# Attention and two expert layers on one core: stores one unit behind, some low parts on VectorE, two scratch tiles in SBUF, value products of a pair in three bursts

## The chip, the cores and the metric

The kernel runs on one core of one Trainium2 chip. The metric is the device time in microseconds (us); lower is better. The median of 3 runs before the change is 1033.18 us (1033.11 to 1035.49).

## The reference

The program is attention with a position bias, then a layer with a rational activation, then a layer with three products and a maximum. Batch 4, 8 heads, sequence 576, head size 64, so 2304 tokens of width 512.

```
scores = q @ k.T / 8 + bias(i, j, head)      # bias: a small two-layer net on log distances
attn   = exp(scores - max) / (sum + 1e-9)
x      = (attn @ v), heads side by side        # 2304 x 512
h      = x @ w_in                              # 2304 x 2048
g      = (a0 + a1 h + a2 h^2 + a3 h^3) / (1 + |b0||h| + |b1|h^2 + 1e-6)
x      = g @ w_out                             # 2304 x 512
h      = max(x @ w1, x @ w2, x @ w3)           # 2304 x 768
out    = h @ w_out2
```

The weights arrive as 64-bit floats and are narrowed on the chip.

## The kernel before

**Precision.** Most products run as three products of high and low parts (`F32R` tiles): ScalarE copies the high part, and GpSimd or VectorE subtracts it from the source to get the low part. A "low part" below is that one subtraction. The value products and the transposes run on plain F32.

**Order.** Nearly all instructions of all engines stand in the order in which the program writes them (`manual_schedule`), so each engine is a queue in order, and so is SP, which issues all DMAs. An instruction that waits holds up what is queued behind it on its engine.

**Stages.** First the bias is computed and stored (to about 70 us). Then the attention stage runs to about 335 us, drains into the first expert layer up to about 372 us, and the two layers follow (to about 745 us and to the end).

**Attention.** A unit is one batch, one pair of heads and one tile of 128 query rows (the fifth tile has 64, and both heads share its products). There are 80 units. A full pair takes five units, in two groups: query tiles 0 and 1, then 2, 3 and 4. The two first pairs of batch 0 run as groups [0], [1], [2] and [3, 4]. `attn_tick(n)` is one step: it issues the score products of unit n (`sc`), a burst of value products of an earlier group (`av`), the transposes of unit n - 2 (`T`), then VectorE's score reductions (`r0`, `r1`), the reciprocal and broadcast (`n`), the store of a finished group (`st`: VectorE multiplies the value bank by the reciprocals into an `xs` tile, and SP stores that to `x_d`), one step of early weight narrowing (`p1`), the splitting of key and query tiles on GpSimd (`sq1` and `sq`, from the list `sqq`), the exponentials (`e0`, `e1`) and the evacuation of the transposes (`v0`, `v1`).

**Value products.** A finished group is queued on `avq` in pieces of its five key blocks, one piece per step, due two steps later. Each key block has a product for each of the two heads, which write 64 partitions each, and each of these shows as two instructions in the trace. The pieces come from `CUT2` for a group of two units (3 and 2 blocks) and from `CUT3` for one of three (2, 2 and 1).

**Banks.** The PSUM tag `bank` has four buffers: the transposes take three of them in a unit, the value products one from their first piece to their store. In the first layer, `ffn_h` takes one for the hidden product `ph`, and `rat_poly` one for its scratch `s`; both are released when VectorE ends the rational function of that step. In the drain of attention, the first steps of the layer and the last units of attention are interleaved.

**Stores.** `attn_store` and `put` (the narrowed weights) issue their DMA on SP in the unit in which VectorE produces the data. `load_kq` and `load_v` for a later pair stand behind them in the same queue. `xs` has four buffers; the narrowed weights use the same tag.

**Low parts.** In `pair_stages`, `rest(i)` takes GpSimd for even and VectorE for odd blocks before the first layer starts. The weight pipeline starts in unit 64. In `split_x`, all low parts are GpSimd's.

Of the kernel before, what the change touches and what calls it, by code (L numbers as in the profile page):

```python
# [17 lines left out]
P = 128  # L18
# [8 lines left out]
HID = 32  # L27
TOFF = 572
TW = 1148
KN = {'AVL': 2, 'NSLOT': 35, 'NRAW': 3, 'NRAWX': 2, 'NATT': 4, 'HB': 0, 'NE': 'd', 'FP': 2, 'BL': 4, 'T4': 0, 'LSP': 1, 'KX': 4, 'HT': 'ss', 'EVP': 'da', 'TTP': 'dda', 'NXS': 4, 'EARLY': 4, 'NM0': 0, 'MAN': 3, 'MANF': 3, 'HA': 2, 'H0': [34, 35], 'L0': [(14, 'k2'), (18, 'v2'), (24, 'k3')], 'B4': 2, 'H2': [1, 2, 4, 6, 8, 10, 12, 14, 16], 'SP0': [3, 4], 'BW': 3, 'A2': ['na', 'sc', 'sq1', 'av', 'T', 'r0', 'r1', 'n', 'st', 'p1', 'p2', 'sq', 'e0', 'e1', 'v0', 'v1'], 'LL': 7, 'SL': 3, 'LL0': 9, 'SL0': 2, 'SQ': [1], 'CUT2': 2, 'CUT3': 3, 'WS': 14, 'WR': 41, 'EV': {None: 'da', 's': 'da', 'j': 'aa'}, 'WT': 64, 'XT': 8, 'XA': 3, 'XB': 8, 'F': ['g2a', 'g2d', 'h', 'g1a', 'w', 'g2p', 'g1d', 'g1p', 'y', 'x', 'g3'], 'LOW': 0, 'LOM': 3, 'LOI': 2, 'GHI': 'dve', 'GLO': 'dve', 'BED': 8, 'BE0': 16, 'NU1': 'pool', 'XE': ['act', 'pool'], 'RS': 3, 'PW': 1, 'WP': 10, 'NPK': 27, 'YSP': 'act', 'LAG': 2, 'EV1': 'dve', 'XSE': 'act', 'STQ': 'sp', 'PUQ': 'sp', 'NB0': 0, 'HP': 0, 'SB': 2, 'XLA': 3, 'XLB': 6, 'XSA': 11, 'YL': 4, 'MIX': [1, 2, 3], 'YN': [(6, 2), (6, 4), (6, 6), (7, 1), (7, 3), (7, 5), (8, 1), (8, 3), (8, 4), (8, 5)], 'WLOW': 1, 'YSN': {5: 2, 6: 2, 7: 1, 8: 1, 9: 1, 10: 1, 11: 1, 12: 1}, 'PLAN': [(2, 1, [0, 2, 3, 4, 5, 6, 7, 8]), (3, 1, [4, 6, 7, 8, 9, 10, 11, 12]), (4, 1, [8, 10, 11, 12, 13, 14, 15, 16]), (5, 2, [1, 3, 5, 6, 8, 10, 12, 14]), (6, 3, [0, 2, 3, 4, 5, 6, 7, 8]), (7, 3, [4, 6, 7, 8, 9, 10, 11, 12]), (8, 3, [8, 10, 11, 12, 13, 14, 15, 16]), (0, 4, [0, 2, 3, 4, 5, 6, 7, 8]), (1, 4, [6, 8, 9, 10, 11, 12, 13, 14])], 'WPN': {13: 1, 14: 1, 15: 1}, 'OB': [1, 5]}  # L30
REBIAS = 2.0 ** -112
TOSIGN = -2.0 ** 32
QC = 1.0 + 1e-6
# [4 lines left out]
def tile_attention_moe(  # L38
# [292 lines left out]
            pool.tensor_copy(*pair)  # L331

    avs = {}

    def attn_v(b, ts, p, js=range(5)):
        n = sum(P if t < 4 else 64 for t in ts)
# [15 lines left out]
    def attn_store(b, ts, p):  # L352
        po = avs.pop((b, ts[0], p))
        n = sum(P if t < 4 else 64 for t in ts)
        xs = sb.tile([P, 512], F32, tag="xs", name=f"xs{b}_{ts[0]}_{p}", bufs=KN['NXS'])
        dve.tensor_tensor(xs[:, :n], po[:, :n], at[b, ts[0], p][1][:, 1, :n], ALU.mult)  # L356
        tok = b * S + ts[0] * P
        (act if KN["STQ"] == "act" else sp).dma_start(x_d[:, p, tok:tok + n], xs[:, :n])


    wt_ = {}
# [17 lines left out]
    def weight_stages(src, name, n, packed=False, lo_eng=pool, narrow=None):  # L379
        box = {}  # L380
        wide_ = src.dtype != F32

        def load():
            if wide_:
                box["r"] = raw(f"wr{name}{n}", [P, 512, 2], I32)
                sp.dma_start(box["r"], src[n].bitcast(I32).rearrange("p (c w) -> p c w", w=2))
            else:
                box["r"] = raw(f"wr{name}{n}", [P, 512], F32)
                sp.dma_start(box["r"], src[n])

        def rebias():
            if wide_:
                low, high = box["r"][:, :, 0], box["r"][:, :, 1]
                act.activation(f32(high), f32(high), AF.Prelu, scale=REBIAS, alpha=TOSIGN)
                dve.tensor_scalar(low, low, 29, None, ALU.logical_shift_right)

        def join():
            if wide_:
                low, high = box["r"][:, :, 0], box["r"][:, :, 1]
                res = sb.tile([P, 512], I32, tag="xs", name=f"wn{name}{n}", bufs=KN['NXS'])  # L400
                dve.scalar_tensor_tensor(res, high, 3, low, ALU.logical_shift_left, ALU.bitwise_or)
                box["r"] = f32(res)

        def put():
            (act if KN["PUQ"] == "act" else sp).dma_start(narrow[n], box["r"])

        def high():
            weight_place(name, n, packed)
            r, w = box["r"], wt_[name, n]
            if isinstance(w, list):  # L410
                for k in range(4):
                    act.copy(w[0][k], r[:, k * P:(k + 1) * P])
            else:
                act.copy(w[:, 0:4].rearrange("p k c -> p (k c)"), r)

        def rest():
            r, w = box["r"], wt_[name, n]
            if isinstance(w, list):
                for k in range(4):
                    lo_eng.tensor_tensor(w[1][k], r[:, k * P:(k + 1) * P], f32(w[0][k]), ALU.subtract)  # L420
            else:
                hi, lo = (w[:, 4 * a:4 * a + 4].rearrange("p k c -> p (k c)") for a in range(2))
                lo_eng.tensor_tensor(lo, r, f32(hi), ALU.subtract)
            ready.add((name, n))

        if narrow is not None:
            return [load, rebias, lambda: (join(), put())]
        return [load, lambda: (rebias(), join()), high, rest]
# [4 lines left out]
    def pair_stages(src, name, n, packed):  # L433
        box = {}

        def load():
            box["r"] = raw(f"wp{name}{n}", [P, 2, 512], F32)
            sp.dma_start(box["r"], src[n:n + 2].rearrange("f p c -> p f c"))

        def high(i):  # L440
            weight_place(name, n + i, packed[i])
            r, w = box["r"][:, i], wt_[name, n + i]
            if isinstance(w, list):
                for k in range(4):
                    act.copy(w[0][k], r[:, k * P:(k + 1) * P])
            else:
                act.copy(w[:, 0:4].rearrange("p k c -> p (k c)"), r)

        def rest(i):
            r, w = box["r"][:, i], wt_[name, n + i]  # L450
            eng = low_eng(KN["LOI"], n + i) if not yps else pool
            if isinstance(w, list):
                for k in range(4):
                    eng.tensor_tensor(w[1][k], r[:, k * P:(k + 1) * P], f32(w[0][k]), ALU.subtract)
            else:
                hi, lo = (w[:, 4 * a:4 * a + 4].rearrange("p k c -> p (k c)") for a in range(2))
                eng.tensor_tensor(lo, r, f32(hi), ALU.subtract)
            ready.add((name, n + i))

        def wait():  # L460
            pass

        return [load] + [wait] * KN["PW"] + [
            lambda: high(0), lambda: (rest(0), high(1)), lambda: rest(1),
        ]

# [26 lines left out]
    def split_x(tag, blk, kc):  # L493
        n = blocks[blk][1]
        rt = xr[tag, blk, kc // 2]
        t = slot(f"{tag}s{blk}_{kc}", [P, 2, n], F32R)
        act.copy(t[:, 0], rt[:, kc % 2])
        pool.tensor_tensor(t[:, 1], rt[:, kc % 2], f32(t[:, 0]), ALU.subtract)  # L498
        xt[tag, blk, kc] = t

    PRODS = ((0, 0), (0, 1), (1, 0))
# [19 lines left out]
    def rat_poly(blk, f):  # L521
        n = blocks[blk][1]
        ph = ph_t[blk, f][:, :n]
        s = bank(f"s{blk}_{f}")[:, :n]
        if blk == 0 and f < KN["RS"]:
            bt = slot(f"g{blk}_{f}", [P, 2, 512], F32)
        else:
            if not gring:
                gring.append(big("gring", [P, 2, 2, 512]))
            bt = gring[0][:, len(gring) % 2]  # L530
            gring.append(None)
        q, u = bt[:, 0, :n], bt[:, 1, :n]
        bun[blk, f] = ph, s, q, u
        act.activation(s, ph, AF.Abs, scale=B0)  # L534
        act.activation(q, ph, AF.Square)  # L535
        dve.scalar_tensor_tensor(q, q, B1, s, ALU.mult, ALU.add)  # L536
        act.activation(u, ph, AF.Identity, scale=A3, bias=A2)  # L537
# [478 lines left out]
    def attn_tick(n):  # L1016
# [9 lines left out]
        for step in KN["A2"]:  # L1026
# [25 lines left out]
            elif step == "av":  # L1052
# [4 lines left out]
                        stq.append(av)  # L1057
                if u2 and u2[2] == u2[1][-1]:
                    av = (u2[0], u2[1], u2[3])
                    cuts = {1: (5,), 2: (3, 2), 3: (2, 2, 1)}  # L1060
                    cut = {1: (5,), 2: cuts[KN["CUT2"]], 3: cuts[KN["CUT3"]]}[len(u2[1])]
                    avq.extend((n + KN["AVL"], av, range(sum(cut[:k]), sum(cut[:k + 1]))) for k in range(len(cut)))
            elif step == "sq1":
# [8 lines left out]
        for b, p in loads_at.get(n, []):  # L1072
            if p % 2 == 0 and (b, p) not in vv:
                load_v(b, p)
            if (b, p) not in raws:
                load_kq(b, p)
        WT, XT = KN["WT"], KN["XT"]
        if WT <= n < NU:
            k = n - WT
# [10 lines left out]
    n = NU  # L1090
    with ordered(KN["MANF"]):
        while avq or stq or n < NU + KN['LAG']:
# [3 lines left out]
            ffn_tick(n - NU, "a")  # L1096
            n += 1
        ffn_tick(n - NU - 1, "b")
    n_drain = n - NU

    with ordered(KN["MANF"]):
# [95 lines left out]
```

## Time and profile before

| | before |
|---|---|
| median of 3 runs | 1033.18 us |
| the profiled execution | 1033.64 us |
| its span, first to last instruction | 1031.9 us |
| TensorE busy | 1000.2 us (97%) |
| VectorE busy | 745.4 us (72%) |
| ScalarE busy | 644.2 us (62%) |
| GpSimd busy | 517.6 us (50%) |
| DMA, mean | 167 GB/s |

The times come from one profiled execution. PE is TensorE, PEld its weight loads, DVE is VectorE, ACT is ScalarE, POOL is GpSimd, and SPq is SP's queue. A row of a timeline gives the start and the length of an instruction (or of several alike), its line in the kernel, what it writes and reads, and in brackets how long the engine sat idle just before, and what ended that.

### The profile page before, as it was taken

How to read it: one execution, taken by the hardware profiler on the slowest of the kernel's cores; microseconds unless marked ns; L12 is line 12 of the kernel's file. 1: busy time of each engine (PE TensorE's matmuls, PEld its weight loads, DVE VectorE, ACT ScalarE, POOL GpSimd, SP SyncE). 2: the span in 40 equal slices, each digit the busy share in tenths (PEclk: the TensorE clock that was granted, in tenths of full speed). 3: DMA queues.
4: the chain of work that ended last, by engine and by line, in shares of the span. 5: the costliest groups of instructions: out<-in, count | busy, mean ns of one | idle time of the engine just before them, and what ended most of it. 6: DMA issues, size and time to landing. Idle time of an engine off the chain costs nothing. (4 is left out here: it accounts for less than half of the span.)

```text
span 1031.9 us, 17512 instructions
## 1 busy us (share of the span) xinstructions
PE 1000.2 (97%) x6082; PEld 821.4 (80%) x6082; DVE 745.4 (72%) x1471; ACT 644.2 (62%) x1294; POOL 517.6 (50%) x691
## 2 busy tenths in 40 slices
PE   6899999999999899999999999999999999999998
PEld 2368767777776678788899788788799999999997
DVE  8976766777676789788889888788775545555544
ACT  8976777877787778777788778778731121131111
POOL 4035677877787354535636356559632641362111
PEclk9999999999999999999999999999999999999999
DMA  7978656565544342023141323323487557745701
GB/s 260 334 265 255 223 193 208 184 223 183 174 146 152 99 147 83 20 93 143 78 168 52 123 93 133 122 92 113 154 314 266 203 178 264 253 130 209 263 31 62
DMA packets 68872, 172.50 MB, mean 167 GB/s; under 512 B 6960, under 2 KB 24624, under 8 KB 68784
## 3 DMA queue, kind: packets, MB, share of 16 engines
q1 hardware_dynamic: 68784, 171.38, 48.0%
q8 instruction: 48, 0.79, 0.3%
q14 instruction: 40, 0.33, 0.1%
HBM read 124.83 MB, written 46.53 MB: 166 GB/s over the span
## 5 line engine op out<-in xcount | busy, mean ns | idle before, releaser
L506 PE MATMUL y<-gs,wwo 128*128 128x512 f32 (+1 forms) x940 | 213.4, 373 | 2.2 <-POOL gs L561 1.9
L506 PE MATMUL ph<-xs,wwi 128*128 128x512 f32 (+1 forms) x930 | 206.8, 370 | 3.0 <-POOL xs L498 1.8
L506 PEld LDWEIGHTS y<-gs,wwo 128*128 128x128 f32 x940 | 164.3, 188 | 37.9 <-POOL gs L561 4.9
L783 PE MATMUL pr<-yo,ws 128*128 128x384 f32 x875 | 190.7, 336 | 2.0 <-DVE m L772 2.0
L506 PEld LDWEIGHTS ph<-xs,wwi 128*128 128x128 f32 x930 | 162.2, 188 | 37.0 <-POOL xs L498 3.6
L561 POOL TENSOR_TENSOR gs<-gring,gs 128x512 fp32r<-128x512 f32 (+1 forms) x77 | 91.1, 1183 | 161.4 <-ACT gs L560 80.3
L783 PEld LDWEIGHTS pr<-yo,ws 128*128 128x128 f32 x875 | 155.4, 188 | 9.5 <-DVE m L772 5.2
L267 ACT ACTIVATE e<-e,st 128x576 f32<-128x576 f32 x144 | 110.8, 772 | 57.1 <-DVE st L261 44.3
L763 POOL TENSOR_TENSOR h<-m,h 128x384 fp32r<-128x384 f32 x36 | 36.7, 1018 | 162.7 <-ACT h L762 144.6
L261 DVE CUSTOM_DVE_ANT_0 e<-s,bias 128x576 f32<-128x576 f32 x144 | 103.6, 752 | 15.6 <-PE s L235 10.1
L534 ACT ACTIVATE s<-ph,keep 128x512 f32<-128x512 f32 (+1 forms) x80 | 49.5, 619 | 72.9 <-PE ph L506 72.5
L235 PE MATMUL s<-k,qs 128*128 128x288 f32 x512 | 84.9, 307 | 2.6 <-DVE st L261 1.4
L308 PEld LDWEIGHTS tp<-ident,e 128*128 128x128 f32 x564 | 60.5, 141 | 31.4 <-issue 11.3
L830 PE MATMUL o<-wmo,h 128*128 128x512 f32 x324 | 82.8, 393 | 0.0
L798 ACT COPY u<-pr 128x384 f32<-128x384 f32 x27 | 12.9, 479 | 109.1 <-PE pr L783 109.1
L308 PE MATMUL tp<-ident,e 128*128 128x128 f32 x564 | 78.5, 280 | 0.8 <-ACT at L1045 0.8
L350 PE MATMUL av<-at,v 128*64 128x320 f32 (+3 forms) x576 | 76.7, 391 | 1.7 <-DVE xs L356 1.1
L536 DVE SCALAR_TENSOR_TENSOR gring<-gring,keep,s 128x512 f32<-128x512 f32 (+1 forms) x77 | 53.0, 689 | 32.4 <-ACT gring L535 31.9
L235 PEld LDWEIGHTS s<-k,qs 128*128 128x128 f32 x512 | 70.3, 189 | 6.1 <-DVE st L261 3.3
L830 PEld LDWEIGHTS o<-wmo,h 128*128 128x128 f32 x324 | 60.1, 188 | 9.7
L548 DVE SCALAR_TENSOR_TENSOR gring<-gring,keep,s 128x512 f32<-128x512 f32 (+1 forms) x77 | 53.2, 691 | 16.6 <-ACT s L542 12.7
L191 PE MATMUL pb<-h,keep 128*32 128x288 f32 x576 | 48.4, 435 | 13.3 <-ACT bo L197 6.1
(168 smaller groups left out, 1895.4 us busy)
## 6 DMA issues: line engine op xcount, KB each, us to landing
ws<-ms_d SPq DMA_DIRECT2D x75, 512.0 KB, 4.8
ms_d<-wring SPq DMA_DIRECT2D x21, 512.0 KB, 2.6
bias_d<-bo SPq DMA_DIRECT2D x36, 288.0 KB, 6.7
kr<-in_k SPq DMA_DIRECT2D x16, 576.0 KB, 5.3
qr<-in_q SPq DMA_DIRECT2D x16, 576.0 KB, 5.7
bias<-bias_d SPq DMA_DIRECT2D x16, 576.0 KB, 6.1
nr<-in_m SPq DMA_DIRECT2D x18, 512.0 KB, 4.6
wrwin<-in_wi SPq DMA_DIRECT2D x16, 512.0 KB, 4.1
```

The costliest lines, as they stand in the source:

```text
L235: pe.matmul(pt[:, x, :HS], lhsT=qs[:, u, t * P:(t + 1) * P], rhs=ks[u][:, w, x * HS:(x + 1) * HS], start=w == 0, stop=w == 1,)
L261: dve.tensor_tensor_reduce(out=dst, in0=src, in1=bs, op0=ALU.add, op1=ALU.min, scale=-0.125, scalar=3.0e38, accum_out=st[:, u:u + 1],)
L267: act.activation(et[:, u], et[:, u], AF.Exp, bias=st[:, u:u + 1], scale=-1.0, accum_out=st[:, 2 + u:3 + u])
L308: pe.transpose(tp[:, j * P:(j + 1) * P], flat[:, 640 * u + j * P:640 * u + (j + 1) * P], ident)
L350: pe.matmul(po[r, :n], lhsT=l, rhs=m, start=j == 0, stop=j == 4, skip_group_check=True)
L506: pe.matmul(po, lhsT=wpart(key, a, k), rhs=rhs, start=first and i == 0, stop=last and i == 2)
L534: act.activation(s, ph, AF.Abs, scale=B0)
L536: dve.scalar_tensor_tensor(q, q, B1, s, ALU.mult, ALU.add)
L548: dve.scalar_tensor_tensor(u, u, A0, s, ALU.add, ALU.mult)
L561: pool.tensor_tensor(t[1], u, f32(t[0]), ALU.subtract)
L783: pe.matmul(pt, lhsT=w[:, a, ch * P:ch * P + P], rhs=ys[c][ch], start=ch == 0 and i == 0, stop=ch == 1 and i == 2,)
L830: pe.matmul(po, lhsT=h[:, a, (tt % 3) * P:(tt % 3 + 1) * P], rhs=mo_t[j][:, c], start=j == 0 and i == 0, stop=j == NF2 - 1 and i == 2,)
```

## The change

- `CUT2` goes from 2 to 1, and `CUT3` from 3 to 4, with a new entry in the table of cuts: a two-unit group is issued as one piece of 5 blocks, a three-unit group as pieces of 4, 0 and 1.
- `attn_store` and `put` no longer issue their DMA at once. They append it to `put_off`; `put_flush`, at the end of each `attn_tick`, issues the DMAs of the unit before and moves those of this unit to `put_due`.
- `rest(i)` uses VectorE while `sqq` still holds key and query splits, whatever the block's number.
- In `split_x`, the low part of block 0, part 3 goes to VectorE.
- In `rat_poly`, the scratch `s` of the first two steps (`RX` = 2) of block 0 is an SBUF tile of tag `xs`, not a bank.

```diff
-KN = {'AVL': 2,
+KN = {'RX': 2, 'AVL': 2,
...
-'CUT2': 2, 'CUT3': 3,
+'CUT2': 1, 'CUT3': 4,
...
+    put_off, put_due = [], []
+
+    def put_flush():
+        while put_due:
+            put_due.pop(0)()
+        put_due.extend(put_off)
+        put_off.clear()
...
     def attn_store(b, ts, p):
...
-        (act if KN["STQ"] == "act" else sp).dma_start(x_d[:, p, tok:tok + n], xs[:, :n])
+        put_off.append(lambda: sp.dma_start(x_d[:, p, tok:tok + n], xs[:, :n]))
...
         def put():
-            (act if KN["PUQ"] == "act" else sp).dma_start(narrow[n], box["r"])
+            put_off.append(lambda: sp.dma_start(narrow[n], box["r"]))
...
         def rest(i):
-            eng = low_eng(KN["LOI"], n + i) if not yps else pool
+            eng = pool if yps else dve if sqq else low_eng(KN["LOI"], n + i)
...
     def split_x(tag, blk, kc):
-        pool.tensor_tensor(t[:, 1], rt[:, kc % 2], f32(t[:, 0]), ALU.subtract)
+        (dve if blk == 0 and kc == 3 else pool).tensor_tensor(t[:, 1], rt[:, kc % 2], f32(t[:, 0]), ALU.subtract)
...
     def rat_poly(blk, f):
-        s = bank(f"s{blk}_{f}")[:, :n]
+        if blk == 0 and f < KN["RX"]:
+            s = sb.tile([P, 512], F32, tag="xs", name=f"s{blk}_{f}", bufs=KN['NXS'])
+        else:
+            s = bank(f"s{blk}_{f}")[:, :n]
...
-                    cuts = {1: (5,), 2: (3, 2), 3: (2, 2, 1)}
+                    cuts = {1: (5,), 2: (3, 2), 3: (2, 2, 1), 4: (4, 0, 1), 5: (5,)}
...
             if (b, p) not in raws:
                 load_kq(b, p)
+        put_flush()
...
+    put_flush()
+    put_flush()
     n_drain = n - NU
```

## Rows read from the trace of the kernel before

**Rows 1.** The page's busy time, share of the span and instructions of TensorE

```profile
PE 1000.2 (97%) x6082; PEld 821.4 (80%) x6082; DVE 745.4 (72%) x1471; ACT 644.2 (62%) x1294; POOL 517.6 (50%) x691
```

**Rows 2.** Busy by stretch: length, each engine's us (instructions), clock, DMA share, GB/s

```profile
71.50:116.00 44.50, 43.66 (x417) 38.12 (x417) 29.59 (x85) 32.42 (x80) 27.48 (x57) 1.00 0.74 241
116.00:195.00 79.00, 76.48 (x574) 57.63 (x571) 55.18 (x141) 59.27 (x145) 59.44 (x110) 1.00 0.57 196
195.00:300.00 105.00, 105.00 (x801) 80.77 (x798) 76.06 (x202) 82.51 (x197) 80.92 (x155) 1.00 0.55 184
300.00:335.00 35.00, 32.48 (x241) 23.73 (x239) 23.42 (x62) 27.56 (x66) 25.87 (x44) 1.00 0.44 145
```

**Rows 3.** Timeline of TensorE: two successive starts of score products, no value products between

```profile
68.43 1.31 PE L235 MATMUL s<-k,qs 128*128 128x288 f32 x8
...
70.58 1.30 PE L235 MATMUL s<-k,qs 128*128 128x288 f32 x8
```

**Rows 4.** Timeline of TensorE: score products, value bursts and the transposes behind them

```profile
285.48 1.30 PE L235 MATMUL s<-k,qs 128*128 128x288 f32 x8
...
300.17 1.52 PE L350 MATMUL av<-at,v 128*64 128x256 f32 x12
301.61 0.66 PE L308 MATMUL tp<-ident,e 128*128 128x128 f32 x4
...
302.24 1.30 PE L235 MATMUL s<-k,qs 128*128 128x288 f32 x8
303.47 0.65 PE L350 MATMUL av<-at,v 128*64 128x256 f32 x4
...
304.49 1.09 PE L308 MATMUL tp<-ident,e 128*128 128x128 f32 x8
...
305.55 1.30 PE L235 MATMUL s<-k,qs 128*128 128x288 f32 x8
```

**Rows 5.** Timeline of TensorE, 150 to 350 us: instructions behind which a wait stands

```profile
151.81 0.33 PE L315 MATMUL tt<-ident,rb 128*128 128x128 f32 x1 [1.20 <-POOL rb L278]
...
154.05 1.30 PE L350 MATMUL av<-at,v 128*64 128x320 f32 x8 [0.85 <-DVE xs L356]
...
314.17 0.33 PE L315 MATMUL tt<-ident,rb 128*128 128x128 f32 x1 [1.15 <-POOL rb L278]
...
327.53 1.30 PE L350 MATMUL av<-at,v 128*64 128x320 f32 x8 [0.47 <-ACT at L1045]
...
339.44 0.73 PE L506 MATMUL ph<-xs,wwi 128*128 128x512 f32 x2 [1.56 <-POOL xs L498]
...
347.26 3.06 PE L506 MATMUL ph<-xs,wwi 128*128 128x512 f32 x12 [1.05 <-DVE g L550]
```

**Rows 6.** Timeline of SP's queue before the query load for batch 1, pair 2

```profile
134.40 0.38 SPq L386 DMA_DIRECT2D wrwin<-in_wi  x1
139.50 0.32 SPq L405 DMA_DIRECT2D wi_n<-wnwin  x1
...
142.05 0.38 SPq L129 DMA_DIRECT2D qr<-in_q  x1
```

**Rows 7.** Timeline of GpSimd where that query load lands

```profile
149.84 1.04 POOL L140 TENSOR_SCALAR qs<-qr 128x1024 fp32r<-128x1024 f32 x1 [4.06 <-DMA qr<-in_q]
```

**Rows 8.** Line 457, the weight low parts: min/median/max ns, first and last start

```profile
L457 POOL TENSOR_TENSOR wwi<-wpwi,wwi x8: 1275/1285/1317, 290.4 to 361.5; 128x512 fp32r<-128x512 f32 x8
...
L457 DVE TENSOR_TENSOR wwi<-wpwi,wwi x6: 680/686/1737, 293.0 to 347.1; 128x512 fp32r<-128x512 f32 x6
...
L457 DVE TENSOR_TENSOR wwo<-wpwo,wwo x2: 1289/1378/1468, 299.9 to 312.5; 128x512 fp32r<-128x512 f32 x2
```

**Rows 9.** Groups by line: ScalarE's exponentials and evacuation (busy us, mean ns, idle before)

```profile
L267 ACT ACTIVATE e<-e,st 128x576 f32<-128x576 f32 x144 | 110.8, 772 | 57.1 <-DVE st L261 44.3 <-POOL qtail L155 5.8 <-DVE st L276 3.2
...
L1045 ACT COPY at<-tp 128x512 f32<-128x512 f32 x78 | 44.8, 575 | 3.9 <-PE av L350 2.5 <-PE tp L308 0.3
...
L267 ACT ACTIVATION_READ_ACCUMULATOR e<-e,st 128x1 f32 x144 | 27.2, 189 | 0.0
```

More of the change, by code (lines that the diff above doesn't have):

```diff
@@ L29 @@
 TW = 1148
-KN = {'AVL': 2, 'NSLOT': 35, 'NRAW': 3, 'NRAWX': 2, 'NATT': 4, 'HB': 0, 'NE': 'd', 'FP': 2, 'BL': 4, 'T4': 0, 'LSP': 1, 'KX': 4, 'HT': 'ss', 'EVP': 'da', 'TTP': 'dda', 'NXS': 4, 'EARLY': 4, 'NM0': 0, 'MAN': 3, 'MANF': 3, 'HA': 2, 'H0': [34, 35], 'L0': [(14, 'k2'), (18, 'v2'), (24, 'k3')], 'B4': 2, 'H2': [1, 2, 4, 6, 8, 10, 12, 14, 16], 'SP0': [3, 4], 'BW': 3, 'A2': ['na', 'sc', 'sq1', 'av', 'T', 'r0', 'r1', 'n', 'st', 'p1', 'p2', 'sq', 'e0', 'e1', 'v0', 'v1'], 'LL': 7, 'SL': 3, 'LL0': 9, 'SL0': 2, 'SQ': [1], 'CUT2': 2, 'CUT3': 3, 'WS': 14, 'WR': 41, 'EV': {None: 'da', 's': 'da', 'j': 'aa'}, 'WT': 64, 'XT': 8, 'XA': 3, 'XB': 8, 'F': ['g2a', 'g2d', 'h', 'g1a', 'w', 'g2p', 'g1d', 'g1p', 'y', 'x', 'g3'], 'LOW': 0, 'LOM': 3, 'LOI': 2, 'GHI': 'dve', 'GLO': 'dve', 'BED': 8, 'BE0': 16, 'NU1': 'pool', 'XE': ['act', 'pool'], 'RS': 3, 'PW': 1, 'WP': 10, 'NPK': 27, 'YSP': 'act', 'LAG': 2, 'EV1': 'dve', 'XSE': 'act', 'STQ': 'sp', 'PUQ': 'sp', 'NB0': 0, 'HP': 0, 'SB': 2, 'XLA': 3, 'XLB': 6, 'XSA': 11, 'YL': 4, 'MIX': [1, 2, 3], 'YN': [(6, 2), (6, 4), (6, 6), (7, 1), (7, 3), (7, 5), (8, 1), (8, 3), (8, 4), (8, 5)], 'WLOW': 1, 'YSN': {5: 2, 6: 2, 7: 1, 8: 1, 9: 1, 10: 1, 11: 1, 12: 1}, 'PLAN': [(2, 1, [0, 2, 3, 4, 5, 6, 7, 8]), (3, 1, [4, 6, 7, 8, 9, 10, 11, 12]), (4, 1, [8, 10, 11, 12, 13, 14, 15, 16]), (5, 2, [1, 3, 5, 6, 8, 10, 12, 14]), (6, 3, [0, 2, 3, 4, 5, 6, 7, 8]), (7, 3, [4, 6, 7, 8, 9, 10, 11, 12]), (8, 3, [8, 10, 11, 12, 13, 14, 15, 16]), (0, 4, [0, 2, 3, 4, 5, 6, 7, 8]), (1, 4, [6, 8, 9, 10, 11, 12, 13, 14])], 'WPN': {13: 1, 14: 1, 15: 1}, 'OB': [1, 5]}
@@ new lines @@
+KN = {'RX': 2, 'AVL': 2, 'NSLOT': 35, 'NRAW': 3, 'NRAWX': 2, 'NATT': 4, 'HB': 0, 'NE': 'd', 'FP': 2, 'BL': 4, 'T4': 0, 'LSP': 1, 'KX': 4, 'HT': 'ss', 'EVP': 'da', 'TTP': 'dda', 'NXS': 4, 'EARLY': 4, 'NM0': 0, 'MAN': 3, 'MANF': 3, 'HA': 2, 'H0': [34, 35], 'L0': [(14, 'k2'), (18, 'v2'), (24, 'k3')], 'B4': 2, 'H2': [1, 2, 4, 6, 8, 10, 12, 14, 16], 'SP0': [3, 4], 'BW': 3, 'A2': ['na', 'sc', 'sq1', 'av', 'T', 'r0', 'r1', 'n', 'st', 'p1', 'p2', 'sq', 'e0', 'e1', 'v0', 'v1'], 'LL': 7, 'SL': 3, 'LL0': 9, 'SL0': 2, 'SQ': [1], 'CUT2': 1, 'CUT3': 4, 'WS': 14, 'WR': 41, 'EV': {None: 'da', 's': 'da', 'j': 'aa'}, 'WT': 64, 'XT': 8, 'XA': 3, 'XB': 8, 'F': ['g2a', 'g2d', 'h', 'g1a', 'w', 'g2p', 'g1d', 'g1p', 'y', 'x', 'g3'], 'LOW': 0, 'LOM': 3, 'LOI': 2, 'GHI': 'dve', 'GLO': 'dve', 'BED': 8, 'BE0': 16, 'NU1': 'pool', 'XE': ['act', 'pool'], 'RS': 3, 'PW': 1, 'WP': 10, 'NPK': 27, 'YSP': 'act', 'LAG': 2, 'EV1': 'dve', 'XSE': 'act', 'STQ': 'sp', 'PUQ': 'sp', 'NB0': 0, 'HP': 0, 'SB': 2, 'XLA': 3, 'XLB': 6, 'XSA': 11, 'YL': 4, 'MIX': [1, 2, 3], 'YN': [(6, 2), (6, 4), (6, 6), (7, 1), (7, 3), (7, 5), (8, 1), (8, 3), (8, 4), (8, 5)], 'WLOW': 1, 'YSN': {5: 2, 6: 2, 7: 1, 8: 1, 9: 1, 10: 1, 11: 1, 12: 1}, 'PLAN': [(2, 1, [0, 2, 3, 4, 5, 6, 7, 8]), (3, 1, [4, 6, 7, 8, 9, 10, 11, 12]), (4, 1, [8, 10, 11, 12, 13, 14, 15, 16]), (5, 2, [1, 3, 5, 6, 8, 10, 12, 14]), (6, 3, [0, 2, 3, 4, 5, 6, 7, 8]), (7, 3, [4, 6, 7, 8, 9, 10, 11, 12]), (8, 3, [8, 10, 11, 12, 13, 14, 15, 16]), (0, 4, [0, 2, 3, 4, 5, 6, 7, 8]), (1, 4, [6, 8, 9, 10, 11, 12, 13, 14])], 'WPN': {13: 1, 14: 1, 15: 1}, 'OB': [1, 5]}
```

## The prediction

> **What bounds the kernel now.** First the page's busy times: TensorE is busy for 97% of the span [rows 1]. Then the busy times by stage [rows 2]: between 71.5 and 335 us, the attention stage, TensorE is busy for 257.6 of 263.5 us, while VectorE, ScalarE and GpSimd stand at 62 to 79%. So what TensorE is given to do sets the time there, and only two things shorten it: less time per unit on TensorE, and fewer waits of TensorE. The reader should see that the stage isn't uniform: in 195 to 300 us TensorE never rests (105.00 of 105.00), in 116 to 195 it rests 2.5 us and in 300 to 335 another 2.5 [rows 2]. After 372 us nothing is edited, and I let that part shift as a whole.
>
> Third, TensorE's timeline, from the start of one unit's score products to the start of the next. A unit without value products takes 2.15 us (68.43 to 70.58) [rows 3]. A unit with eight value instructions of 256 columns takes 3.31 us (302.24 to 305.55). Its burst lasts 1.02 us (303.47 to 304.49), and a burst of twelve lasts 1.44 us (300.17 to 301.61), so one instruction adds (1.44 - 1.02) / 4 = 0.105 us [rows 4]. Eight of them are 0.84 us, and 3.31 - 2.15 - 0.84 leaves **0.32 us that each burst costs whatever its length**. It is paid going from the 128-column form to the 64-column form and back, and it counts as busy.
>
> Fourth, the waits of TensorE [rows 5]: 1.20 and 0.85 us at 151 to 154; five waits from 314.17 to 327.53 (the first and the last stand there; 1.15, 0.23, 0.30, 0.34 and 0.47, together 2.49 us); 1.56 us at 339.44; 1.05 us at 347.26.
>
> **The change part by part.** *Bursts.* A full pair has 5 units and, today, 5 bursts (3+2 key blocks for the two-unit group, 2+2+1 for the three-unit group). With one cut of 5 and cuts of 4, 0 and 1 it has 3; the empty one issues nothing. 14 full pairs save 2 bursts each, and the two early pairs save 1 each in their last group: 30 bursts. 30 x 0.32 = 9.6 us. The columns stay. Where TensorE sets the pace all of that is gained; where it already waits for others I count half. The stretches 71.5 to 116 and 195 to 300 are 149.5 of 263.5 us, the other two 114 [rows 2], so (149.5 + 114 / 2) / 263.5 = 0.78, and 0.78 x 9.6 = 7.5 us. Bounds: half of it, 4.8, to all, 9.6.
>
> *The uneven units that come with it.* Following the queue of bursts, the unit of query tile 1 now has all five blocks (20 instructions), that of tile 2 none, tile 3 four blocks, tile 4 none, and the next tile 0 the last block. About 28 units are thus as short as 2.15 us. No row shows such a unit in mid-stage, so I bound what it loses. Below: nothing, as in rows 3, where a short unit ran without a wait. Above: it lasts as long as ScalarE's work of a unit, 2 x (0.772 + 0.189) + 2 x 0.575 = 3.07 us [rows 9], 0.92 us more, 28 x 0.92 = 25.8 us in all. I stay near the lower end. The short unit always stands beside one with 16 or 20 value instructions, in which ScalarE and VectorE catch up before the transposes. In the tile 2 unit no value bank is held, so its three transpose banks have a fourth beside them; the tile 4 unit has one exponential instead of two. A long burst also frees the transposed tile a unit earlier than today. I take 2.0 us lost (0.07 us for each).
>
> *Stores one unit behind.* SP is a queue in order. At 139.50 it issues the narrow-weight store for which it had waited on VectorE, and only then the loads of v, k and q; the q load goes out at 142.05 [rows 6]. GpSimd waits 4.06 us for it, until 149.84 [rows 7], then runs late, and TensorE waits 1.20 us for GpSimd's broadcast and 0.85 us for what VectorE does behind that [rows 5]. With that store and the attention stores a unit later, their data is long there when SP reaches them, and the loads queued behind them follow what SP issued at 134.40 [rows 6] or the release of their buffer, which the rows don't separate. Each microsecond earlier up to 2.05 counts. Bounds 0 to 2.05; I take 1.5. What now waits instead is the store's buffer: four tiles, under one new one per unit, each held one unit longer (3.3 us). I cost that at nothing; VectorE's multiply would wait if a fifth were wanted early.
>
> *Low parts on VectorE.* Three weight low parts fall in units in which key and query splits are queued (67, 71 and 72) and leave GpSimd, 1.28 us each. On VectorE they took 0.69 us, or 1.29 to 1.47 in two cases [rows 8]. VectorE is busy 23.4 of 35 us there [rows 2], so it has room, but they stand ahead of the next unit's score reduction. GpSimd's broadcast is what is late at 314.17 [rows 5]. Bounds for the five waits: from 1.0 us worse (three long low parts, a third of each on the path) to 2.49 better; I take 1.0. The fourth is the low part of the last x tile of the first block. TensorE waits 1.56 us for it at 339.44 [rows 5], since GpSimd does a weight low part of 1.28 us first. VectorE is free once ScalarE has written the high part. Bounds 0 to 1.56; I take 0.8, because it may hit a long 1.3 us case.
>
> *The first two rational steps in SBUF.* At 347.26 the third hidden product waits 1.05 us for VectorE to release a bank [rows 5]; two steps hold four banks beside the value products. Two scratch tiles leave the banks, and so does the value tile, one unit sooner. What is late next is the low part of the first activated tile for the first output product. Bounds 0 to 1.05; I take 0.8. The four VectorE operations with that scratch I cost at nothing, hidden beside a hidden product; without that cover they lose up to 0.78 us each (1.47 - 0.69 [rows 8]).
>
> The Trainium skill speaks against these two edits. By its page "SBUF — State Buffer" (Who interferes with whom), a VectorE instruction with two SBUF inputs and a GpSimd instruction that reads SBUF exclude each other for their whole length. The 1.47 us case agrees with that, the 0.69 us median doesn't, and the rows don't show what ran beside either. By the rule alone these two parts would gain nothing.
>
> *Sum.* 7.5 + 1.5 + 1.0 + 0.8 + 0.8 = 11.6 us gained, 2.0 lost, 9.6 net. The profiled execution took 1033.64 us (span 1031.9); 1033.64 - 9.6 = 1024.0. The median of the runs is 0.46 below the profiled one, so **1023.6 us**.
>
> **The rivals.** *A, slower: the short unit is paced by ScalarE.* Then the transposes of the short units wait for evacuations. At the full 3.07 us the 28 units lose 25.8 us, against 11.6 gained: 14.2 us slower, 1047. It decides against the change from 11.6 / 28 = 0.41 us per short unit. For it: ScalarE is busy 79% in 300 to 335 [rows 2], and conversions come on top. Against it: the neighbouring long units and the short unit of rows 3. *B, absorbed: the slack of the others is smaller than their busy shares suggest,* since they wait for each other in order. Then bursts pay only in 195 to 300 us, 105 / 263.5 x 9.6 = 3.8 us, and the waits stay: 1029.4. For it: TensorE already waits in both neighbouring stretches. Against: those waits have causes of their own [rows 5 to 7]. *C, the two units compared differ by more than a burst,* so that the 0.32 us isn't removed. Then only the waits pay, 4.1 - 2.0 = 2.1 us: 1031.1. Against it: the burst alone already has 1.02 - 0.84 = 0.18 us that don't grow with its length [rows 4]. *D, low parts and scratch exclude GpSimd:* the last three terms, 2.6 us, are lost: 1026.2.
>
> **How the numbers follow.** Forecast, a gain of 5 to 16 us: 0.70. A 0.08, B 0.11, C 0.05, D 0.06. A measurement of this kernel can't tell 0.3% (3.1 us) from no change. The forecast and D are faster; of B and C together, 0.09 is faster and 0.07 the same; of A, 0.06 is slower, and 0.02 is the same; that makes faster 0.85, same 0.09, slower 0.06. The range: all bounds at their best give 9.6 + 2.05 + 2.49 + 1.56 + 1.05 = 16.8 us, 1016.4; I set the low end at 1017.5. The high end takes in B and just about C: 1031.
>
> **What would show it.** The value bursts of the attention stage number 50, not 80, and a full pair takes 16.1 us, not 16.76 (285.48 to 302.24 [rows 4]). Units without value products last 2.15 to 2.3 us; at 2.6 or more, A is at work. The q loads go out sooner behind the units' stores, GpSimd's waits for them shrink, and the waits at 151 to 154 go. The first hidden product runs through with at most 0.8 us of waiting, and the third starts without VectorE. The stage from 372 us on keeps its length. The prediction is wrong if transposes or scores wait in the short units, or if a full pair takes as long as before.

## The result, and the profile after

| | before | after |
|---|---|---|
| median | 1033.18 us | 1023.0 us (1020.06 to 1024.71) |
| profiled execution | 1033.64 us | 1020.06 us |
| its span | 1031.9 us | 1018.2 us |

The ratio is 0.9889 (95% interval 0.9869 to 0.9908): 1.1% faster. (The two medians alone give 0.9901, inside that interval.) The same kernel beside other runs of before gave 1020.72 us and 0.9865 (0.9843 to 0.9887). The forecast was 1023.6 us. The profiled execution is the fastest of its five, so its trace shows 13.6 us where the medians show 10.2.

The page's busy times of the changed kernel answer [rows 1]:

```profile
PE 991.0 (97%) x6082; PEld 823.6 (81%) x6082; DVE 750.0 (74%) x1475; ACT 644.1 (63%) x1294; POOL 514.9 (51%) x687
```

TensorE has 9 us less of busy time for the same 6082 instructions. The busy times by stage answer [rows 2]; the stage ends 10 us sooner, so the last two stretches are moved by that:

```profile
71.50:116.00 44.50, 44.50 (x430) 39.77 (x428) 30.20 (x86) 32.48 (x79) 28.14 (x59) 1.00 0.71 239
116.00:195.00 79.00, 78.22 (x611) 61.62 (x607) 60.41 (x155) 64.04 (x156) 62.53 (x118) 1.00 0.65 211
195.00:290.00 95.00, 95.00 (x751) 76.68 (x750) 70.59 (x188) 76.34 (x184) 76.02 (x143) 1.00 0.57 188
290.00:325.00 35.00, 33.07 (x248) 25.50 (x244) 26.50 (x66) 30.17 (x71) 26.66 (x45) 1.00 0.47 152
```

In 116 to 195 us TensorE now rests 0.8 us instead of 2.5 and issues 611 instructions instead of 574. TensorE's timeline in mid-stage answers [rows 3, 4]:

```profile
234.26 1.40 PE L246 MATMUL s<-k,qtail 128*128 128x288 f32 x10
...
243.73 1.30 PE L235 MATMUL s<-k,qs 128*128 128x288 f32 x8
...
250.53 1.41 PE L246 MATMUL s<-k,qtail 128*128 128x288 f32 x10
...
257.06 1.95 PE L357 MATMUL av<-at,v 128*64 128x256 f32 x16
258.84 0.60 PE L357 MATMUL av<-att,vz 128*64 128x256 f32 x4
...
260.00 1.30 PE L235 MATMUL s<-k,qs 128*128 128x288 f32 x8
...
262.14 1.04 PE L235 MATMUL s<-k,qs 128*128 128x288 f32 x6
```

A full pair takes 16.27 us (243.73 to 260.00, or 234.26 to 250.53 between the score products of tile 4) instead of 16.76 [rows 4]. The unit after the five-block burst starts at 260.00 and the next at 262.14: a short unit of 2.14 us in mid-stage, as long as that of [rows 3].

A yardstick for all runs below: the starts of the tile 4 score products (line 246) give the lengths of the 14 full pairs, from the second early pair to the last one.

| kernel | ratio to before (95%) | 14 pairs, us | inner 11, us | disturbed pairs of the inner 11 |
|---|---|---|---|---|
| before | 1 | 241.4 | 189.3 | 5 (17.16 to 19.18; undisturbed 16.76) |
| changed kernel | 0.9889 (0.9869 to 0.9908) | 230.0 | 180.9 | 1 (17.82; undisturbed 16.2 to 16.3) |
| cuts alone | 1.0009 (0.9994 to 1.0024) | 242.0 | 188.0 | 5 (17.14 to 18.57) |
| stores alone | 0.9958 (0.9944 to 0.9971) | 236.8 | 184.6 | none |
| cuts and stores | 0.9926 (0.9910 to 0.9942) | 233.0 | 180.9 | 1 (17.97) |
| changed, stores at once | 0.9962 (0.9947 to 0.9976) | 239.3 | 188.7 | 6 (16.74 to 18.58) |

The inner ones leave out the first two, which still hold bursts of the early pairs, and the last; a pair counts as disturbed from about 0.35 us above the undisturbed length. The lengths come from one trace of each kernel; a gain in us that stands beside a ratio is worked out from that ratio.

Of the 13.6 us between the profiled executions, 11.5 lie in these 14 pairs. About 0.8 lies ahead of them: the first scores start at 61.77 instead of 62.80, and in 50 to 71.5 us the granted clock of the execution before was 0.92, that after 1.00. The edits act behind that part, and in the second trace of the changed kernel the first scores start at 62.67. About 1.3 lie behind the last scores.

### The profile page after: what moved, and what is told of

Same layout as the page of the kernel before. It is cut to its first block, busy times and chain, and to the rows that moved or that the text cites. A ratio compares the mean times of both kernels' runs of the same rounds, so it can differ in the third digit from the quotient of the medians.

```text
span 1018.2 us, 17475 instructions
## 1 busy us (share of the span) xinstructions
PE 991.0 (97%) x6082; PEld 823.6 (81%) x6082; DVE 750.0 (74%) x1475; ACT 644.1 (63%) x1294; POOL 514.9 (51%) x687
## 5 line engine op out<-in xcount | busy, mean ns | idle before, releaser
L261 DVE CUSTOM_DVE_ANT_0 e<-s,bias 128x576 f32<-128x576 f32 x144 | 103.8, 752 | 13.6 <-PE s L246 8.9
L357 PE MATMUL av<-at,v 128*64 128x320 f32 (+3 forms) x576 | 70.1, 385 | 0.0
```

The source lines that it names most:

```text
L261: dve.tensor_tensor_reduce(out=dst, in0=src, in1=bs, op0=ALU.add, op1=ALU.min, scale=-0.125, scalar=3.0e38, accum_out=st[:, u:u + 1],)
L357: pe.matmul(po[r, :n], lhsT=l, rhs=m, start=j == 0, stop=j == 4, skip_group_check=True)
```

## The experiments

**Is a burst worth something by itself?** The kernel before with the cuts alone.

```diff
-'CUT2': 2, 'CUT3': 3,
+'CUT2': 1, 'CUT3': 4,
```

> The kernel before with the cuts 5 and 4, 0, 1 alone. Theory (each burst costs TensorE a constant beside its columns): a full pair goes from 16.76 to about 16.25 us where TensorE sets the pace, 14 pairs, so 6 to 8 us faster, about 1026, and the waits of TensorE at 151 to 154 and after 314 us stay. Rival (the gain comes from the earlier loads, and the cuts only shift columns): within 2 us of before. Rival A (short units paced by ScalarE): slower than before, short units of 2.6 us and more.

Measured: 1035.6 us beside 1034.88, 0.1% slower, with an interval that holds no change. The cuts alone give nothing. Undisturbed pairs did fall to 16.2 us, but others rose to 17 to 18.6. TensorE's waits in its timeline:

```profile
115.19 0.33 PE L315 MATMUL tt<-ident,rb 128*128 128x128 f32 x1 [1.60 <-POOL rb L278]
...
123.32 0.33 PE L315 MATMUL tt<-ident,rb 128*128 128x128 f32 x1 [1.00 <-POOL rb L278]
...
259.96 0.33 PE L315 MATMUL tt<-ident,rb 128*128 128x128 f32 x1 [1.00 <-POOL rb L278]
```

In the trace of the kernel before, no wait for that broadcast stands at any of these three places. Ahead of the third, SP's queue:

```profile
235.17 0.38 SPq L386 DMA_DIRECT2D wrwon<-in_wo  x1
240.89 0.32 SPq L405 DMA_DIRECT2D wo_n<-wnwon  x1
241.31 0.38 SPq L121 DMA_DIRECT2D v<-in_v  x1
241.78 0.41 SPq L127 DMA_DIRECT2D kr<-in_k  x1
242.40 0.33 SPq L129 DMA_DIRECT2D qr<-in_q  x1
```

and GpSimd's timeline:

```profile
249.41 1.05 POOL L140 TENSOR_SCALAR qs<-qr 128x1024 fp32r<-128x1024 f32 x1 [2.32 <-DMA qr<-in_q]
```

It is the pattern of [rows 6, 7] at another place: SP stands for 5.7 us in front of a store of narrowed weights, then issues v, k and q at once; GpSimd waits 2.32 us for q, runs late with its splits, and its broadcast for TensorE comes late behind them. The inner 11 pairs lose 9.7 us against an undisturbed length of 16.21, where before they lost 4.9 against 16.76: that takes back most of the 6.0 us that the bursts save in them. That a shorter pair leaves less time for the loads is the likely reason, but it is argued: GpSimd's own waits for the query loads are no longer than before (8.5 us instead of 9.8 in 71 to 335 us), while TensorE's waits for GpSimd's broadcast grow from 2.3 us to 5.2.

**What are the earlier loads worth?** The kernel before with only the stores one unit behind.

```diff
...
-        (act if KN["STQ"] == "act" else sp).dma_start(x_d[:, p, tok:tok + n], xs[:, :n])
+        put_off.append(lambda: sp.dma_start(x_d[:, p, tok:tok + n], xs[:, :n]))
...
-            (act if KN["PUQ"] == "act" else sp).dma_start(narrow[n], box["r"])
+            put_off.append(lambda: sp.dma_start(narrow[n], box["r"]))
...
+        put_flush()
...
```

> The kernel before with only the stores one unit behind. Theory: GpSimd's waits for the query loads (9.8 us in all) shrink to about 1 us and TensorE's waits at 151 to 154 (2.05 us) go; 1.5 to 2 us faster, about 1031.5; the length of a full pair elsewhere stays 16.76 us. Rival (the loads are the main gain): 5 us or more. Rival (loads are hidden anyway): 0.

Measured: 1030.96 beside 1034.88, 0.42% faster (4.4 us), three times the forecast. In 71 to 335 us GpSimd waits for no query load any more. Pairs that were disturbed now have the undisturbed length; from its timeline:

```profile
155.38 1.40 PE L246 MATMUL s<-k,qtail 128*128 128x288 f32 x10
...
172.14 1.40 PE L246 MATMUL s<-k,qtail 128*128 128x288 f32 x10
```

That is 16.76 us. The pair at the same place in the kernel before:

```profile
156.34 1.40 PE L246 MATMUL s<-k,qtail 128*128 128x288 f32 x10
...
163.64 1.48 PE L235 MATMUL s<-k,qs 128*128 128x288 f32 x8 [0.23 <-DVE st L261]
...
173.97 1.40 PE L246 MATMUL s<-k,qtail 128*128 128x288 f32 x10
```

It took 17.63 us, and the 0.23 us in brackets is all the waiting that is shown in it. The brackets miss much of what a pair loses; its length doesn't.

**Do the cuts pay on top of the stores?** Both edits, nothing else.

> The kernel before with the cuts and the stores one unit behind, nothing else. Alone the cuts gave 0.0% and the stores 0.4%. Theory (the cuts shorten a pair by 0.5 us only if GpSimd gets the keys and queries in time, which the early loads give): the two together give about 4.4 + 6.5 us less the late wait at 312 and 314, so 9 to 10.5 us, about 1025 beside 1034.9; full pairs of 16.2 to 16.3 us. Rival (the parts add): 4.4 us, 1030.5.

Measured: 1027.42 beside 1034.89, ratio 0.9926. The cuts that gave nothing alone give 0.3% more on top of the stores (0.9958 to 0.9926); the 14 pairs fall from 236.8 to 233.0. That is 7.7 us in all (6.0 to 9.3 by the interval): the rival (4.4 us) is out, but the 9 to 10.5 us weren't reached either. The trace says where they are missing:

```profile
302.07 1.40 PE L246 MATMUL s<-k,qtail 128*128 128x288 f32 x10
...
306.80 0.33 PE L315 MATMUL tt<-ident,rb 128*128 128x128 f32 x1 [1.19 <-POOL rb L278]
...
323.32 1.40 PE L246 MATMUL s<-k,qtail 128*128 128x288 f32 x10
...
332.28 0.73 PE L514 MATMUL ph<-xs,wwi 128*128 128x512 f32 x2 [2.13 <-POOL xs L506]
```

The last pair takes 21.25 us, and the x part is waited for 2.13 us: the late stretch, in which the weight low parts load GpSimd. With the low parts on VectorE, in the changed kernel, the same pair:

```profile
299.36 1.43 PE L246 MATMUL s<-k,qtail 128*128 128x288 f32 x10
...
301.57 0.66 PE L308 MATMUL tp<-ident,e 128*128 128x128 f32 x4 [0.29 <-ACT at L1055]
...
302.25 1.30 PE L235 MATMUL s<-k,qs 128*128 128x288 f32 x8
...
309.40 1.30 PE L235 MATMUL s<-k,qs 128*128 128x288 f32 x8
...
312.20 1.48 PE L235 MATMUL s<-k,qs 128*128 128x288 f32 x8 [0.40 <-DVE st L261]
...
317.52 1.40 PE L246 MATMUL s<-k,qtail 128*128 128x288 f32 x10
```

18.16 us, 3.1 less.

**Which store holds the loads up?** As the run before, but the narrowed weights are stored at once and only the attention stores wait a unit.

```diff
-            put_off.append(lambda: sp.dma_start(narrow[n], box["r"]))
+            (act if KN["PUQ"] == "act" else sp).dma_start(narrow[n], box["r"])
```

> As the run before, but only the attention stores go one unit behind; the stores of the narrowed weights are issued at once. Theory (the query loads stand behind the narrowed store in the same unit, as at 139.5 us before): most of the waits of the cuts alone come back up to 260 us, pairs of 17 to 18.5 us, about 1030. Rival (the attention stores hold the loads up): as the run before, about 1025.

Measured: 1032.31 beside 1034.89, ratio 0.9977 (0.9963 to 0.9991), 14 pairs of 241.0 us: most of the gain is gone, and pairs of 17.05 to 18.6 us are back. What waited for whom in 71 to 335 us (total, times, longest):

```profile
POOL qs L140 <- DMA qr<-in_q: 7.4, 5, 3.7
...
PE tt L315 <- POOL rb L278: 4.3, 5, 1.2
```

In the changed kernel the first of these is 1.2 us in all and the second doesn't occur. So the loads stand above all behind the store of the narrowed weights, as long as weights are narrowed. A kernel with only that store late wasn't run, so what the attention stores add isn't shown.

**The changed kernel without the late stores.**

> The changed kernel with the stores issued at once, as before. If the parts simply add, it is 1.5 to 2 us slower than the changed kernel (about 1025). If shorter units make the loads more urgent, more than that: 3 us or more, with GpSimd's waits for the query loads well above the 9.8 us of before.

Measured: 1031.35 beside 1034.94, ratio 0.9962. Taking the late stores out costs 0.7 to 1.0% (against 0.9889 and 0.9865), 7.5 to 10 us, where they gave 4.4 us alone. The parts don't add: the stores are what lets the cuts pay. GpSimd's waits for the query loads didn't rise well above the 9.8 us of before, as the second case expected (9.1 us); the loss shows in the inner 11 pairs, 188.7 us instead of 180.9.

**What is a burst worth once nothing disturbs the pair?** The changed kernel with four and with two bursts in a full pair.

```diff
-'CUT2': 1, 'CUT3': 4,
+'CUT2': 2, 'CUT3': 4,      # four bursts
+'CUT2': 1, 'CUT3': 5,      # two bursts
```

> The changed kernel with the two-unit group in two pieces of 3 and 2 again: four bursts in a full pair instead of three, 16 more in all. Theory of a constant per burst (0.25 us by the traces of before and after: 0.5 us per pair for two bursts): 4 us slower than the changed kernel, about 1027. Rival (the lumping, not the number, matters): no change or faster, since its units are more even.

> The changed kernel with the three-unit group in one piece of 5: two bursts in a full pair. Theory of a constant per burst: 14 fewer, 3.5 us faster than the changed kernel, about 1019.5. Rival A (three short units behind each other, paced by ScalarE and VectorE): the gain is eaten, 1023 or slower, with TensorE waiting in the units without value products.

Measured: 1024.47 us, ratio 0.9898 (0.9880 to 0.9917), and 1022.77 us, ratio 0.9879 (0.9860 to 0.9897); neither can be told from the changed kernel. The pair lengths can. Four bursts:

```profile
254.52 1.40 PE L246 MATMUL s<-k,qtail 128*128 128x288 f32 x10
...
271.03 1.40 PE L246 MATMUL s<-k,qtail 128*128 128x288 f32 x10
```

Two bursts, with two waits of its late stretch:

```profile
234.44 1.40 PE L246 MATMUL s<-k,qtail 128*128 128x288 f32 x10
...
250.52 1.40 PE L246 MATMUL s<-k,qtail 128*128 128x288 f32 x10
...
293.32 1.47 PE L235 MATMUL s<-k,qs 128*128 128x288 f32 x8 [0.89 <-DVE st L261]
...
311.54 1.46 PE L235 MATMUL s<-k,qs 128*128 128x288 f32 x8 [1.47 <-DVE st L261]
```

An undisturbed pair takes 16.76, 16.51, 16.2 to 16.27 and 16.08 us with five, four, three and two bursts: 0.25 and 0.24 to 0.31 us for each of the first two taken out, some 0.15 for the next. The constant per burst is real. Its sum isn't the gain: with four bursts ten of the 14 pairs run at 16.51 or 16.52 without any disturbance, and with two TensorE waits for VectorE's score reductions in the late stretch, where VectorE does a weight low part ahead of the reduction (1.11 us from 291.48, 1.78 us from 309.03). That isn't rival A, which named ScalarE; its sign there is a wait of 0.78 us for ScalarE's evacuation, at 147.92. The inner 11 pairs take 182.6 us with four bursts and 181.3 with two, against 180.9 with three.

**The low parts alone.**

```diff
-            eng = low_eng(KN["LOI"], n + i) if not yps else pool
+            eng = pool if yps else dve if sqq else low_eng(KN["LOI"], n + i)
```

and the `split_x` line of the change.

> The kernel before with only the low parts on VectorE. By the prediction 1.0 us from the three weight parts and 0.8 us from the x part: 1.8 us faster, 1031.4. After its trace: the x part took 1.46 us on VectorE and TensorE still waited 1.44 us for it, so the x part gains nothing and the whole is 0 to 1.2 us. Rival D (VectorE and GpSimd exclude each other): slower by up to 1 us.

Measured: 1032.69 beside 1034.88, ratio 0.9977 (0.9963 to 0.9991), 2.4 us faster. The last pair takes 18.86 us instead of 20.57, and the wait of 1.15 us at 314.17 [rows 5] is gone. The x part is waited for less too, from its timeline:

```profile
337.78 0.73 PE L506 MATMUL ph<-xs,wwi 128*128 128x512 f32 x2 [0.89 <-DVE xs L498]
```

0.89 us instead of 1.56, so the expectation that the x part gains nothing was wrong. That rival D makes this slower is out.

**The scratch tiles alone.**

> The kernel before with only the two SBUF scratch tiles. By the prediction 0.8 us faster. After its trace (the third hidden product ran without a wait, but the first output product then waited 1.24 us for the low part of the first activated tile): 0 to 0.3 us, the wait of 1.05 us at the third hidden product gone and one of about 1 us at the first output product in its place.

Measured: 1034.86 beside 1034.88, ratio 1.0000 (0.9987 to 1.0013). TensorE's waits at the start of the layer:

```profile
339.39 0.73 PE L506 MATMUL ph<-xs,wwi 128*128 128x512 f32 x2 [1.56 <-POOL xs L498]
...
349.77 2.60 PE L506 MATMUL y<-gs,wwo 128*128 128x512 f32 x10 [0.39 <-POOL gs L564]
```

The wait of 1.05 us at the third hidden product [rows 5] is gone, and one of 0.39 us stands at the first output product. The difference of 0.7 us is smaller than what the time can tell. Beside the cuts the tiles aren't needed for that wait: in the kernel with cuts and stores and no scratch tile, the second and third hidden products already run on without one, and the first output product waits 0.85 us:

```profile
335.88 5.91 PE L514 MATMUL ph<-xs,wwi 128*128 128x512 f32 x24
```

**The start of the first layer.** In the changed kernel TensorE still waits there twice:

```profile
325.80 0.73 PE L513 MATMUL ph<-xs,wwi 128*128 128x512 f32 x2 [1.44 <-DVE xs L505]
...
337.01 2.82 PE L513 MATMUL y<-gs,wwo 128*128 128x512 f32 x11 [1.24 <-POOL gs L571]
```

ScalarE's, VectorE's and GpSimd's timelines ahead of the first of them:

```profile
322.13 1.16 ACT L454 CAST wwi<-wpwi 128x512 fp32r<-128x512 f32 x2
323.17 0.64 ACT L504 CAST xs<-xr 128x512 fp32r<-128x512 f32 x1
```

```profile
323.69 0.68 DVE L329 COPY at<-tw 128x512 f32<-128x512 f32 x1
324.29 1.46 DVE L505 TENSOR_TENSOR xs<-xr,xs 128x512 fp32r<-128x512 f32 x1
```

```profile
323.93 1.27 POOL L464 TENSOR_TENSOR wwi<-wpwi,wwi 128x512 fp32r<-128x512 f32 x1
```

The high part stands behind two weight casts, and the low part takes 1.46 us. I took the late high part for the cause, so I issued the split ahead of the weight step, and in a second kernel also the second half of a layer step ahead of the attention step in the drain.

```diff
+        if NU - 4 <= n < NU:
+            split_x("x", 0, n - NU + 4)
         if WT <= n < NU:
             k = n - WT
...
-            attn_tick(n)
             if n > NU:
                 ffn_tick(n - NU - 1, "b")
+            attn_tick(n)
```

> The changed kernel with the split of the first block's x tiles issued before the weight step of the same unit instead of after it. Theory: the wait of 1.44 us at the first hidden product is set by ScalarE's cast of the last x tile, which stands behind two weight casts (1.16 us), not by which engine does the low part; the wait shrinks to 0.3 us and the time by about 1 us. Rival (VectorE's low part is slow beside GpSimd): the wait stays above 1 us.

> The changed kernel with the x tiles split before the weight step, and with the second half of a layer step issued before the attention step of the same unit in the drain, so that ScalarE's logarithm of the first rational step doesn't stand behind two evacuations. Theory: the wait of 1.24 us at the first output product shrinks to 0.3 us or less, and with the x tiles the time is 1.5 to 2.5 us below the changed kernel, about 1021. Rival (what is gained is waited for at the next output product): 0.5 to 1 us.

Measured: 1021.48 us, ratio 0.9875 (0.9854 to 0.9896), and 1021.45 us, ratio 0.9873 (0.9849 to 0.9896). The waits in the second one:

```profile
326.72 0.73 PE L513 MATMUL ph<-xs,wwi 128*128 128x512 f32 x2 [0.74 <-DVE xs L505]
...
337.14 2.83 PE L513 MATMUL y<-gs,wwo 128*128 128x512 f32 x11 [0.85 <-POOL gs L571]
```

1.44 became 0.74 (0.73 in the first kernel) and 1.24 became 0.85, not the 0.3 us expected of each. The traces speak for the rival of the first kernel's expectation. VectorE and GpSimd in the second one:

```profile
325.39 0.68 DVE L329 COPY at<-tw 128x512 f32<-128x512 f32 x1
325.98 0.68 DVE L505 TENSOR_TENSOR xs<-xr,xs 128x512 fp32r<-128x512 f32 x1
```

```profile
326.36 1.45 POOL L464 TENSOR_TENSOR wwi<-wpwi,wwi 128x512 fp32r<-128x512 f32 x1 [0.69 <-ACT wwi L454]
```

With and without the edit the low part starts right behind VectorE's copy of transposes, and the high part is written before that (at 323.81 in the changed kernel), so the high part wasn't what it waited for. What fell is the low part's length, from 1.46 to 0.68 us in both kernels, now that it begins ahead of GpSimd's weight low part instead of behind it, and the wait fell by about as much. The time can't be told from that of the changed kernel, which ran once more beside the second of the two:

> The changed kernel once more, beside the same runs of before as the others of this call: 1.1% faster, about 1023.5.

Measured: 1020.72 us, ratio 0.9865 (0.9843 to 0.9887). No version here is shown to beat the changed kernel.

## Why the prediction was right, and which terms were not

The time, 1023.6 forecast and 1023.0 measured, hides terms that were off in both directions. The mechanisms were in the sum, but not that the edits work on each other, and that the errors nearly cancel is luck.

- **Bursts, 7.5 us forecast.** The step from rows to a constant per burst held: 0.32 us forecast, 0.24 to 0.31 measured on undisturbed pairs. The step that failed is the one that multiplied it by a fixed share of TensorE-bound time. Alone the cuts give 0.0 us; on top of the stores 0.3%, some 3.3 us. "Where it already waits for others I count half" took those waits as fixed, but with the cuts alone what the inner 11 pairs lose grew from 4.9 to 9.7 us, and with the loads moved forward as well it fell to 2.6 (undisturbed 16.21). Rival B, given 0.11, describes the cuts alone better than the forecast does.
- **Uneven units, 2.0 us lost.** Short units take 2.14 to 2.31 us in undisturbed pairs, as written, and these pairs lose nothing that shows. In the last pair two short units take 2.89 us (299.36 to 302.25) and 2.80 us (309.40 to 312.20), above the 2.6 that the prediction named as a sign of A, some 1.2 us together. A wait of 0.29 us in the first is for ScalarE's evacuation, as A has it; the 0.40 us behind the second is for VectorE. So rival A is out up to 290 us, and a small part of it is there in the last pair.
- **Stores, 1.5 us forecast, bounded at 2.05.** Alone they give 4.4 us. The mechanism was right, a store in front of the loads; the size was wrong, since I took TensorE's bracketed waits at one place as the bound. Pair lengths would have bounded it better: the inner 11 pairs of the kernel before exceed 16.76 by 4.9 us in all.
- **Low parts, 1.0 and 0.8 us.** Alone 2.4 us (0.9 to 3.8 by the interval), within the bounds given. The weight parts carry it: 1.7 us in the last pair alone, 3.1 with cuts and stores there. The x part gained 0.7 us alone (0.89 instead of 1.56) and 0.7 on top of cuts and stores (1.44 instead of 2.13). The prediction's sign, at most 0.8 us of waiting at the first hidden product, didn't come, because the cuts had lengthened that wait: it is 2.13 us with the cuts alone too. In 324.29 to 325.75 VectorE's low part overlaps a GpSimd low part of 1.27 us that began at 323.93. By the Trainium skill, page "SBUF — State Buffer" (Who interferes with whom), the two exclude each other; the 1.46 us beside the 0.69 us median of [rows 8] agrees, which is rival D at this one place. The prediction had allowed for such a long case, of 1.3 us. Its 1.29 to 1.47 us for the long weight parts left out the longest of [rows 8], 1.74 us.
- **Scratch tiles, 0.8 us.** Alone, the wait named went, and what the prediction named as late next took part of its place, 0.39 us: worth nothing that can be measured. With the cuts the wait is gone without the tiles, so in the changed kernel the term counted a wait that another edit removes. The prediction had said that the value tile leaves the banks a unit sooner, but not that this is enough. No run takes only the tiles out of the changed kernel.

In order, then: stores 4.4 us, cuts on top 3.3, low parts and scratch on top of both 3.8 to 6.3 (0.9926 to 0.9889 or 0.9865), where the forecast had 1.5, 5.5 and 2.6. What the cuts were given too much, the stores were given too little; the rest was given too little as well, so by the same ratios the whole is 11.5 to 14.0 us, more than the net of 9.6. The inner 11 pairs tell the same of cuts and stores with less scatter: 1.3 us shorter with the cuts, 4.7 with the stores, 8.4 with both. The low parts and the scratch tiles leave them at 180.9; what these gain lies behind them, 3.1 us in the last pair and 0.7 at the x part.

The runs of the changed kernel spread over 4.7 us where those of before, beside them, spread over 2.4. That isn't the change's doing: the 17 runs of before beside the last four experiments spread over 6.3 us (1031.97 to 1038.28). Part of such a spread lies ahead of the attention stage: the first scores start between 61.59 and 64.70 us in the 14 traces. One thing stays open: the single disturbed pair that is left (17.82 us, from 118 to 136 us; 17.97 with cuts and stores alone). GpSimd waits for no load in it, but VectorE waits 1.75 us, until 123.03, for GpSimd, which splits the query tails first; why GpSimd is late there wasn't found.

## What to carry to other kernels

Before adding up what several edits give, ask which of them only pays if another lands: time taken off the bounding engine can come back as waits if a transfer in an ordered queue isn't moved forward with it. A store that waits for its data in front of loads can cost more than the waits seen where it stands (here 4.4 us against 2.05); put it one step later in the queue. And to bound a stall, compare the lengths of repeated periods with the undisturbed one, rather than sum the idle times of an engine whose instruction ends are modelled.

## What the runs showed of the hardware beyond that

Each burst of 64-column products between 128-column ones cost TensorE about a quarter of a microsecond beside its columns, inside its busy time: from 195 to 290 us TensorE is busy throughout, 95.00 of 95.00 us, with pairs of 16.76 us as with pairs of 16.2 to 16.4. That the change of form is what costs it is argued; the runs vary only the number of bursts.

VectorE's subtraction of a 128x512 low part took 1.46 us when a GpSimd subtraction had begun 0.36 us ahead of it, and 0.68 us when it began ahead of GpSimd's by 0.38 us; GpSimd's then took 1.45 us instead of 1.27.

The granted clock between 50 and 71.5 us, where the bias products run, was 0.92 on the mean in the profiled execution before and 1.00, its upper level, in that after, and the scores began 1.0 us sooner in the second.
